# Seeds of a convolution kernel computed two eighths at a time, beside the attention projections

## The chip, the core and the metric

The kernel runs on one core of a Trainium2 chip. The time is device microseconds of one execution, from three runs. A profile comes from one further execution; its span is measured from the first to the last instruction, and its tables name the engines PE (matrix multiply), PEld (its weight loads), DVE (vector), ACT (scalar, activations), POOL (GpSimd) and SP, which here only issues transfers.

## The reference

The output is two results side by side. The first is an S4D convolution of `u` (2048 x 448) with a kernel made from 448 x 256 complex exponentials; the second is 16-head attention over 2048 positions with width 448.

```python
dt = exp(log_dt); A = -exp(log_A_real) + 1j * A_imag
C = (C_real + 1j * C_imag) * dt[:, None]
P = exp((A * dt[:, None])[:, :, None] * arange(L))
K = 2.0 * einsum("dn,dnl->dl", C, P).real
y = irfft(rfft(u.T, 2 * L) * rfft(K, 2 * L), 2 * L)[:, :, :L].T + u * D_skip
qkv = (x @ wqkv)...                          # H = 16 heads of 28
p = softmax(einsum("bhqd,bhkd->bhqk", q, k) * Dh ** -0.5)
b = einsum("bhqk,bhkd->bhqd", p, v) @ wo
out = concatenate([y, b], axis=-1)
```

## The kernel before

It has a first stage, in which a scheduler orders the instructions of each engine by priority and data, and a main stage, in which every engine keeps the order of the program. The main stage (scores, exponentials, products with `v`, and the convolution's matmuls and powers) is not touched by the change. In it `sdb` is the seeds of a block of 8 channels read back from memory, and each head group's first matmuls need the row maxima in `qhat`.

The first stage does two jobs side by side.

**The projections.** `work` is a list of 48 jobs: for each of four chunks `c` of 512 positions eight `qk_proj` (k and q of four head groups) and four `v_proj`, each 12 matmuls into one of three `pm` tiles. `transposes(c)` makes the four `xh` and `xl` of a chunk: PE transposes into `pt`, ACT copies `xh`, DVE subtracts for `xl`. `evac` empties a `pm` tile: ACT writes `hl`'s first half, DVE the second, and SP stores `hl` to `k` or `q` in memory; for k of the first two chunks `kb` and `dhl` follow on ACT, DVE and POOL, and for v ACT writes one of two `v` staging buffers. `project()` takes one job and first runs the evacuation of the job before, held in `pend`. The projection weights lie in the memory that later holds `khat`, so the `khat` loads follow the projections.

**The seeds.** `seeds(o)` makes the starting values of eighth `o` (of eight) of the exponentials `P`: it returns 13 lists of functions, one a slot. In order: `load` (four `nat` loads), `times_dt` on ACT, `exp_a`, `turn` (eight PE transposes into `pn`, ACT copies `tr`), `phases` (three small DVE operations on `pn`, one product over 128 x 1680 into `tri`, and one on POOL), `reduce` (two more such operations on DVE), `sines` (two sines, an absolute value and two cosines on ACT, into `sg` and `tri`), `sizes` (two exponentials on ACT), `factors` (three POOL operations on `sg`), `g_base` (two small POOL products on `tri`, then a negation on ACT), `e_all` (two POOL products from `tri` into a `qhat` buffer), `g_first` (nine DVE operations), `g_copies` (four small ACT copies), and the stores `put_e` (`sd<-qhat`) and `put_g` (`sd<-sg`). `tri` has two buffers, `sg` two and the `qhat` buffers three.

A loop over slots `t` interleaves both: eighth `o` begins at slot 4 `o` (`SP`), the projections are spread over 37 slots (`PW`), and `ahead` places the first `kdif`, `q` and `khat` loads. The 41 slots set the program order; the scheduler, whose priority follows it, sets the queues. After the loop come 16 steps that find the maxima of the first score tile (ACT `rl`, DVE, with `nq` from POOL), which need all `khat` and both parts of `qhat`; their PSUM tiles take the place of those of the first stage.

ACT needs a table load between a sine and an exponential. SP sends all transfers of this stage in one order; each of them takes one of eight semaphores in turn.

Of the kernel before, what the change touches and what calls it, by code (L numbers as in the profile page):

```python
# [8 lines left out]
F32 = mybir.dt.float32  # L9
F32R = mybir.dt.float32r  # L10
I32 = mybir.dt.int32
AF = mybir.ActivationFunctionType
ALU = mybir.AluOpType
# [25 lines left out]
S0, SP, SW, SD, PW, E3 = 0, 4, 0, 5, 37, 8  # L39
# [2 lines left out]
SGB, XB, XL = 2, 5, 4  # L42
K0, KP, KD, UP = 0, 3.5, 4, 3
A0, A1, KW = 26, 34, (33, 35, 36)

N1 = 32
N2 = 64
# [5 lines left out]
NO = 8  # L53
# [3 lines left out]
NF, NE = 6, 13  # L57
# [5 lines left out]
TWO_PI = 6.283185  # L63
# [28 lines left out]
def body(ctx, tc, a, out):  # L92
    nc = Engines(tc)
# [119 lines left out]
    with ExitStack() as st:  # L213
# [47 lines left out]
        t = a["A_log_dt"]  # L261
# [6 lines left out]
        half_pi = s_p.tile([128, 1], F32, name="half_pi")  # L268
# [42 lines left out]
        NH = BO * 16  # L311
        mul = lambda e, o_, x_, y_: e.tensor_tensor(o_, x_, y_, ALU.mult)

        def seeds(o):

            q = {}
            vec, pol, act = nc.vector, nc.gpsimd, nc.scalar
# [1 line left out]
            kb = lambda i: pw2[:, i, :, None].to_broadcast([128, LV, NH])  # L319

            def exp_a():
                act.activation(q["nat"][:, 0, :], q["nat"][:, 0, :], AF.Exp)

            def times_dt(i):
                n, d = q["nat"][:, i, :], dt_all[:, i or 4, o:o + 1]
                act.activation(n, n, AF.Copy, scale=d)
# [37 lines left out]
                q["g4"] = sg[:, :, :F_Z - F_G].rearrange("p b (c h e) -> p b c h e", c=2, e=4)  # L364
                q["f"] = sg[:, :, F_Z - F_G:].rearrange("p b (t k h) -> p t k b h", t=3, h=16)

            def both(t, i, *args, **kw):
                act.activation(q["f"][:, i], t[:, :NF].rearrange("p k (b h) -> p k b h", h=16), *args, **kw)
                act.activation(t[:, NF:], t[:, NF:], *args, **kw)

            def sines():
                f = q["f"][:, 2]
                act.activation(f, q["r"][:, :NF].rearrange("p k (b h) -> p k b h", h=16), AF.Sin, scale=TWO_PI)
                act.activation(q["sn"][:, NF:], q["r"][:, NF:], AF.Sin, scale=TWO_PI)
                act.activation(q["r"], q["r"], AF.Abs)
                both(q["r"], 0, AF.Sin, scale=-TWO_PI, bias=half_pi)

            def sizes():
                both(q["mg"], 1, AF.Exp)

            def factors():
                f = q["f"]
# [37 lines left out]
            put_e = lambda: nc.sync.dma_start(sd_d[o][:, :, :F_G].rearrange("b p f -> p b f"), q["se"])  # L420
            put_g = lambda: nc.sync.dma_start(sd_d[o][:, :, F_G:].rearrange("b p f -> p b f"), q["sg"])

            def load():
                if o not in nats:
                    load_nat(o)
                q["nat"] = nats.pop(o)
            dts = lambda *r: [lambda i=i: times_dt(i) for i in r]
            return [[load], dts(1, 2, 3), [], [exp_a] + dts(0), [turn, phases], [g_place, reduce], [sines], [sizes, places, g_base],
                    [e_all, g_first], [put_e, factors], [g_copies], [], [put_g]]

        xh, xl = {}, {}

        def transposes(c):
            for k in range(NCK):
                pt = ps_t.tile([128, CQ], F32, name="pt")[:CK]
                for t in range(4):
                    nc.tensor.transpose(pt[:, t * 128:(t + 1) * 128], xns[c, t // 2][:, t % 2, k * CK:(k + 1) * CK], ident)
                xh[k] = x_p.tile([CK, CQ], F32R, name="xh", bufs=XB)
                xl[k] = x_p.tile([CK, CQ], F32R, name="xl", bufs=XL)
                nc.scalar.activation(xh[k], pt, AF.Copy)  # L440
                nc.vector.tensor_tensor(xl[k], pt, xh[k].bitcast(F32), ALU.subtract)

        def qk_proj(c, s, g):
            pp = w_tile()
# [46 lines left out]
        for c in range(NQ):  # L491
            jobs = [lambda c=c, s=s, g=g: qk_proj(c, s, g) for g in range(G) for s in (1, 0)]
            v_jobs = [lambda c=c, t=t: v_proj(c, t) for t in range(4)]
            jobs = v_jobs + jobs if c == NQ - 1 else jobs + v_jobs
            jobs[0] = (lambda c, f: lambda: (transposes(c), f())[1])(c, jobs[0])
            if c + 1 < NQ:
                jobs[1] = (lambda c, f: lambda: (load_x(c + 1), f())[1])(c, jobs[1])
            work += jobs
        stages = [seeds(o) for o in range(NO)]
        n_stage = SP * (NO - 1) + len(stages[0])  # L500
        slots = [[] for _ in range(n_stage)]
        for o in range(NO):
            for i, st_ in enumerate(stages[o]):
                slots[max(SP * o + (i or -2), 0)] += st_
        slots[1].insert(0, turn_dt)
        pend, n_work = [], len(work)

# [9 lines left out]
        def project():  # L517

            e = work.pop(0)() if work else None
            while pend:  # L520
                pend.pop(0)()
            if e:
                pend.append(e)

        for t in range(n_stage):
            while work and n_work - len(work) < n_work * (t + 1) / PW:
                project()
            for f in slots[t] + ahead.get(t, []):
                f()
            if t + 1 == PW:  # L530
                project()
                wst.close()
                load_k(0, HG - 1, k0_p)
                load_q(1)
                for c in range(NQ):
                    load_v(0, c)
# [6 lines left out]
        for i in range(16):  # L543
            j, t = divmod(i, 4)
            ts = slice(t * 128, (t + 1) * 128)
            q, kt = q_u[0][:, j, ts], kt_g[0][j]
# [201 lines left out]
    def fin(u, s_):  # L748
# [15 lines left out]
        def scale():  # L764
            pw = w_tile()
            for t in range(4):
                nc.tensor.transpose(pw[:, t * 128:(t + 1) * 128], rb[:, t].rearrange("p h e -> p (h e)"), ident)
            nc.vector.tensor_tensor(on, o, pw, ALU.mult)
            if g < G - 1:
                nc.sync.dma_start(on_d[c][g], on)  # L770
            else:
                p_due.extend((s_ + PD + PS * t, lambda t=t: project(t)) for t in range(4))
# [385 lines left out]
```

## Time and profile before

| | us |
|---|---|
| three runs | 1304.3, 1303.38, 1303.45 (median 1303.45) |
| the profiled execution | 1307.74 |
| its span | 1305.7 |
| granted TensorE clock, mean | 0.976 |
| PE busy | 1228.7 (94%) |
| ACT busy | 980.3 (75%) |
| DVE busy | 907.0 (69%) |
| POOL busy | 865.9 (66%) |

Nearly all instructions are recorded at line 76, where a wrapper calls the engine, so groups are told apart by tile names: `pm` projection PSUM, `hl` and `kb` their evacuations, `tri`, `sg` and `pn` the seeds, `sd` the seeds in memory. A row of the timeline gives start, duration, engine, operation, output and inputs, and, where the engine had been idle, for how long and on whom it waited. A row of a group gives total busy time and the mean of one in ns, then the idle time before them. A row of the list of waits gives the total in us, the number of waits and the longest.

### The profile page before, as it was taken

Reading aid. Unit: us, or ns where it says so; the run is one execution under the profiler, and the core shown is the slowest. Engines: PE = TensorE matmul, PEld = TensorE weight load, DVE = VectorE, ACT = ScalarE, POOL = GpSimd, SP = SyncE. Lnnn points to the kernel's source line nnn. Section 1 sums busy time; section 2 is a strip of 40 time slices with the busy share of each in tenths; the row PEclk is TensorE's granted clock in tenths of the full one; section 3 lists DMA queues with packets and bytes.
Section 4 is the critical chain, followed back from the end, with each engine's and each line's share of the span. In section 5 each row is a group of like instructions: output and inputs, shape, how many; then the busy total and the mean of one; then the engine's idle time right before and its main releaser. Section 6 shows DMA issues by size and latency. Waiting matters only on the chain.

```text
span 1305.7 us, 32148 instructions
## 1 busy us (share of the span) xinstructions
PE 1228.7 (94%) x12193; PEld 695.7 (53%) x12193; DVE 907.0 (69%) x2001; ACT 980.3 (75%) x2046; POOL 865.9 (66%) x684
## 2 busy tenths in 40 slices
PE   6888877799999999999999999999997999999998
PEld 5766755355555555555555555555554555545333
DVE  5676656677777787777788888888986555636111
ACT  4877875588888888888788888888886666756463
POOL 2677654478888788888769999999995221424421
PEclk9989887799999999999999999999999999999999
DMA  6677679735866455468634232743324453647666
GB/s 202 207 273 257 218 259 271 212 66 136 185 147 142 109 149 157 142 169 231 162 104 105 56 83 62 157 111 78 82 59 139 146 158 136 203 142 238 202 161 175
DMA packets 200082, 205.28 MB, mean 157 GB/s; under 512 B 95992, under 2 KB 158520, under 8 KB 197880
## 3 DMA queue, kind: packets, MB, share of 16 engines
q1 hardware_dynamic: 199864, 203.22, 56.1%
q8 instruction: 96, 1.57, 0.5%
q14 instruction: 58, 0.48, 0.1%
q10 hardware_dynamic: 64, 0.02, 0.0%
HBM read 120.74 MB, written 82.18 MB: 155 GB/s over the span
## 4 chain that ended last, share of the span: by engine, by line
PE 72%; POOL 8%; ACT 7%; DVE 5%; DMA 4%; issue 4%; SPq 0%; ACTq 0%; POOLq 0%
PE pm L76 39%; PE pss L76 16%; PE po L76 16%; POOL sg L76 2%; POOL e L76 2%; DMA khat<-k 2%; POOL tri L76 2%; ACT tri L76 1%; ACT sg L76 1%; DVE mx L76 1%; POOL p L76 1%; ACT L76 1%; ACT p L76 1%; POOL eu L76 1%; DVE rl L76 1%
## 5 line engine op out<-in xcount | busy, mean ns | idle before, releaser
L76 ACT ACTIVATE p<-pss 128x512 f32<-128x512 f32 x1024 | 560.4, 609 | 109.9 <-PE pss L76 105.9
L76 PE MATMUL pss<-qhat,khat 128*128 128x512 f32 x1024 | 405.7, 402 | 4.0 <-DMA qhat<-mh 2.2
L76 DVE TENSOR_REDUCE mx<-pm 128x1 f32<-128x512 f32 x480 | 308.3, 683 | 121.2 <-PE pm L76 119.5
L76 PE MATMUL pm<-khat,qhat 128*128 128x512 f32 x720 | 314.4, 437 | 6.1 <-ACT rl L76 3.5
L76 POOL TENSOR_TENSOR e<-e,sdb 128x256 f32<-128x256 f32 x168 | 202.0, 1203 | 108.7 <-ACT e L76 67.2
L76 PE MATMUL po<-p,v 128*32 128x512 f32 x2048 | 271.0, 597 | 0.0
L76 POOL TENSOR_TENSOR e<-e,eu 128x256 f32<-128x256 f32 x168 | 248.3, 1478 | 13.2
L76 PEld LDWEIGHTS pm<-khat,qhat 128*128 128x128 f32 x720 | 135.4, 188 | 206.4 <-ACT p L76 47.0
L76 PEld LDWEIGHTS pss<-qhat,khat 128*128 128x128 f32 x1024 | 191.2, 189 | 52.5 <-ACT p L76 13.8
L76 DVE CUSTOM_DVE_ANT_0 rl<-pm,rl 128x512 f32<-128x512 f32 x240 | 165.3, 689 | 70.0 <-ACT rl L76 67.7
L76 POOL TENSOR_TENSOR eu<-e,sdb 128x256 f32<-128x256 f32 x168 | 202.3, 1204 | 0.0
L76 POOL TENSOR_TENSOR p<-pr,pr 64x448 f32<-64x448 f32 x64 | 73.2, 1144 | 155.6 <-PE pm L76 122.3
L76 DVE TENSOR_TENSOR g<-g,zg 128x128 f32<-128x128 f32 x392 | 162.0, 413 | 3.6
L76 ACT ACTIVATE rl<-pm 128x512 f32<-128x512 f32 x240 | 145.3, 605 | 7.7 <-issue 4.1
L76 PE MATMUL pm<-xh,khat 112*128 112x512 f32 x256 | 89.7, 431 | 19.6 <-DVE hl L76 10.6
L76 PE MATMUL pm<-kdif,qhat 128*128 128x512 f32 x240 | 97.0, 404 | 1.7 <-DVE pr L76 1.1
L76 DVE TENSOR_TENSOR zg<-g,zg 128x128 f32<-128x128 f32 x224 | 88.0, 393 | 5.3
L76 PEld LDWEIGHTS pm<-e,g 128*32 128x32 f32 x3584 | 56.9, 110 | 49.2 <-issue 15.7
L76 PE MATMUL pm<-e,g 128*32 128x64 f32 x3584 | 73.6, 223 | 8.7 <-POOL e L76 8.7
L76 ACT ACTIVATE y<-pm 128x448 f32<-128x448 f32 x48 | 26.5, 553 | 59.7 <-PE pm L76 39.1
L76 PEld LDWEIGHTS pm<-xh,khat 112*128 112x128 f32 x256 | 51.0, 205 | 35.9 <-DVE hl L76 12.6
L76 DVE TENSOR_TENSOR pr<-pm,ub 128x448 f32<-128x448 f32 x64 | 37.0, 619 | 46.9 <-PE pm L76 37.7
(133 smaller groups left out, 1491.6 us busy)
## 6 DMA issues: line engine op xcount, KB each, us to landing
sdb<-sd SPq DMA_DIRECT2D x56, 336.0 KB
khat<-k SPq DMA_DIRECT2D x64, 256.0 KB
qhat<-q SPq DMA_DIRECT2D x64, 256.0 KB
sd<-sg SPq DMA_DIRECT2D x8, 1456.0 KB
k<-hl SPq DMA_DIRECT2D x16, 512.0 KB
q<-hl SPq DMA_DIRECT2D x16, 512.0 KB
v<-v SPq DMA_DIRECT2D x32, 256.0 KB
mw<-in_mw SPq DMA_DIRECT2D x16, 512.0 KB
```

Source lines behind the costliest of these rows:

```text
L76: i = f(*args, **kw)
```

## The change

Four edits, all in the first stage.

Eighths now begin in pairs, at slots 0 and 1, 8 and 9, 16 and 17, 24 and 25; there are 38 slots in place of 41. Within an eighth the steps `g_place`, `places`, `sizes`, `g_first` and `put_g` change slots.

`in_group(g, i)` gives ACT's sines and exponentials numbers: `exp_a` of both eighths of pair p is group 3p, their sines and cosines 3p + 1, their `sizes` 3p + 2. Each instruction of a group gets an edge of order, without a semaphore, to every instruction of the group before it.

`transposes` issues `xh` and `xl` with a priority raised by 200, and so does `project()` with the pending evacuation. Nothing is computed otherwise than before.

```diff
+PRI = 200
...
+        groups = collections.defaultdict(list)
+        def in_group(g, i):
+            for b in groups[g - 1]:
+                tc.add_manual_dep(i.ins, b.ins.name, mybir.DependencyInfo(mybir.DependencyClass.NoSync, mybir.DependencyReason.DATA),
+                                  reason="one function table at a time")
+            groups[g].append(i)
...
-                act.activation(q["nat"][:, 0, :], q["nat"][:, 0, :], AF.Exp)
+                in_group(3 * (o // 2), act.activation(q["nat"][:, 0, :], q["nat"][:, 0, :], AF.Exp))
...
-            def both(t, i, *args, **kw):
-                act.activation(q["f"][:, i], t[:, :NF].rearrange("p k (b h) -> p k b h", h=16), *args, **kw)
-                act.activation(t[:, NF:], t[:, NF:], *args, **kw)
+            def both(n, t, i, *args, **kw):
+                g = 3 * (o // 2) + n
+                in_group(g, act.activation(q["f"][:, i], t[:, :NF].rearrange("p k (b h) -> p k b h", h=16), *args, **kw))
+                in_group(g, act.activation(t[:, NF:], t[:, NF:], *args, **kw))
...
-                act.activation(f, q["r"][:, :NF].rearrange("p k (b h) -> p k b h", h=16), AF.Sin, scale=TWO_PI)
-                act.activation(q["sn"][:, NF:], q["r"][:, NF:], AF.Sin, scale=TWO_PI)
+                in_group(g, act.activation(f, q["r"][:, :NF].rearrange("p k (b h) -> p k b h", h=16), AF.Sin, scale=TWO_PI))
+                in_group(g, act.activation(q["sn"][:, NF:], q["r"][:, NF:], AF.Sin, scale=TWO_PI))
                 act.activation(q["r"], q["r"], AF.Abs)
-                both(q["r"], 0, AF.Sin, scale=-TWO_PI, bias=half_pi)
+                both(1, q["r"], 0, AF.Sin, scale=-TWO_PI, bias=half_pi)
...
-                both(q["mg"], 1, AF.Exp)
+                both(2, q["mg"], 1, AF.Exp)
...
-            return [[load], dts(1, 2, 3), [], [exp_a] + dts(0), [turn, phases], [g_place, reduce], [sines], [sizes, places, g_base],
-                    [e_all, g_first], [put_e, factors], [g_copies], [], [put_g]]
+            return [[load], dts(1, 2, 3), [], [exp_a] + dts(0), [turn, phases], [reduce], [g_place, sines], [places], [sizes, g_base],
+                    [e_all], [put_e, factors, g_first], [g_copies], [put_g]]
...
-                nc.scalar.activation(xh[k], pt, AF.Copy)
-                nc.vector.tensor_tensor(xl[k], pt, xh[k].bitcast(F32), ALU.subtract)
+                with tc.high_priority(offset=PRI):
+                    nc.scalar.activation(xh[k], pt, AF.Copy)
+                    nc.vector.tensor_tensor(xl[k], pt, xh[k].bitcast(F32), ALU.subtract)
...
-        n_stage = SP * (NO - 1) + len(stages[0])
+        begin = [2 * SP * (o // 2) + o % 2 for o in range(NO)]
+        n_stage = begin[-1] + len(stages[0])
...
-                slots[max(SP * o + (i or -2), 0)] += st_
+                slots[max(begin[o] + (i or -2), 0)] += st_
...
-            while pend:
-                pend.pop(0)()
+            with tc.high_priority(offset=PRI):
+                while pend:
+                    pend.pop(0)()
```

More of the change, by code (lines that the diff above doesn't have):

```diff
@@ L365, in g_place @@
                 q["f"] = sg[:, :, F_Z - F_G:].rearrange("p b (t k h) -> p t k b h", t=3, h=16)
-            def both(t, i, *args, **kw):
-                act.activation(q["f"][:, i], t[:, :NF].rearrange("p k (b h) -> p k b h", h=16), *args, **kw)
-                act.activation(t[:, NF:], t[:, NF:], *args, **kw)
+            def both(n, t, i, *args, **kw):
+                g = 3 * (o // 2) + n
+                in_group(g, act.activation(q["f"][:, i], t[:, :NF].rearrange("p k (b h) -> p k b h", h=16), *args, **kw))
+                in_group(g, act.activation(t[:, NF:], t[:, NF:], *args, **kw))
             def sines():
-                f = q["f"][:, 2]
-                act.activation(f, q["r"][:, :NF].rearrange("p k (b h) -> p k b h", h=16), AF.Sin, scale=TWO_PI)
-                act.activation(q["sn"][:, NF:], q["r"][:, NF:], AF.Sin, scale=TWO_PI)
+                f, g = q["f"][:, 2], 3 * (o // 2) + 1
+                in_group(g, act.activation(f, q["r"][:, :NF].rearrange("p k (b h) -> p k b h", h=16), AF.Sin, scale=TWO_PI))
+                in_group(g, act.activation(q["sn"][:, NF:], q["r"][:, NF:], AF.Sin, scale=TWO_PI))
                 act.activation(q["r"], q["r"], AF.Abs)
-                both(q["r"], 0, AF.Sin, scale=-TWO_PI, bias=half_pi)
+                both(1, q["r"], 0, AF.Sin, scale=-TWO_PI, bias=half_pi)
             def sizes():
-                both(q["mg"], 1, AF.Exp)
+                both(2, q["mg"], 1, AF.Exp)
             def factors():
```

## The prediction

> **What bounds the kernel now.** I read the page's head first, then the windows of busy time, the chain of waits around 240 us, the list of who waited for whom up to there, and last the timelines of single queues.
>
> ```profile
> span 1305.7 us, 32148 instructions
> 0.00:208.00 208.00, 164.68 (x706) 128.74 (x707) 133.41 (x218) 146.46 (x254) 124.71 (x103) 0.92 0.73 237
> 208.00:242.00 34.00, 26.79 (x86) 17.31 (x84) 21.78 (x39) 16.91 (x17) 5.28 (x4) 0.80 1.00 286
> 245.00:1305.00 1060.00, 1035.16 (x11398) 548.18 (x11397) 751.81 (x1745) 816.91 (x1775) 735.90 (x578) 0.99 0.52 137
> ```
>
> A window row gives its length, the busy time of PE, weight loads, DVE, ACT and POOL, then the granted clock, the DMA share and GB/s. From 245 us on PE is busy 1035 of 1060 us. That part keeps its program order on every engine, so I carry it over unchanged: the change is worth what it does to the moment at which that part can start. In the first 208 us no engine is full (PE 79%, ACT 70%, DVE 64%, POOL 60%): something hands work round among them. Between 208 and 242 the DMA engines are: share 1.00 at 286 GB/s.
>
> ```profile
> 218.32 10.46 DMA khat<-k
> 236.38 5.56 DMA qhat<-mh
> 242.00 2.99 DMA sdb<-sd
> ...
> 232.66 0.37 SPq L76 DMA_DIRECT2D sd<-qhat  x1
> 233.82 0.37 SPq L76 DMA_DIRECT2D sd<-sg  x1
> ```
>
> The chain says the same: the main loop starts at 245 when the first `sdb` has landed. That load was issued at 242.00, once the last seed store (sent at 233.82, behind the `khat`, `qhat` and `v` loads in SP's queue) had landed. The score maxima reach their row of `qhat` at 241.9, so two paths end together. Both hang on a backlog of transfers that begins when the last seeds and projections are done.
>
> ```profile
> DVE hl L76 <- ACT hl L76: 27.5, 14, 5.3
> DVE sg L76 <- POOL tri L76: 23.2, 7, 5.5
> ACT tri L76 <- POOL tri L76: 21.4, 11, 3.7
> ...
> 33.55 1.91 DVE L76 TENSOR_TENSOR tri<-pn,pw 128x1680 f32<-128x1680 f32 x1
> ...
> 78.83 1.91 DVE L76 TENSOR_TENSOR tri<-pn,pw 128x1680 f32<-128x1680 f32 x1
> ...
> 121.69 1.91 DVE L76 TENSOR_TENSOR tri<-pn,pw 128x1680 f32<-128x1680 f32 x1
> ...
> 162.34 1.89 DVE L76 TENSOR_TENSOR tri<-pn,pw 128x1680 f32<-128x1680 f32 x1
> ```
>
> Two things wait in those 208 us. Projection evacuations wait for ScalarE (27.5 us), and the seeds' chain goes DVE, ACT, POOL, DVE. The four starts are eighths 0, 2, 4 and 6; the gaps are 45.3, 42.9 and 40.7 us for two eighths, which overlap because they are half a period apart.
>
> **The change part by part.** *Table loads.* ScalarE's queue has 17 now and 9 after.
>
> ```profile
> L76 ACT ACT_TABLE_LOAD x17 | 21.8, 1283 | 1.0 <-PEq L1148 0.7
> ...
> 170.82 0.77 ACT L76 ACTIVATE sg<-tri 128x672 f32<-128x672 f32 x1
> ...
> 175.73 1.12 ACT L76 ACTIVATE tri<-tri,half_pi 128x1008 f32<-128x1008 f32 x1
> ...
> 201.43 0.56 DVE L76 TENSOR_TENSOR sg<-pn,tri 128x224 f32<-128x224 f32 x1 [2.12 <-POOL tri L76]
> ...
> 205.06 0.55 DVE L76 TENSOR_TENSOR sg<-sg,px 128x224 f32<-128x224 f32 x1
> ```
>
> That frees 8 x 1.283 = 10.3 us of ScalarE. But ScalarE idles 21.4 us for POOL's `tri`, so this counts only where ScalarE's sequence sets the pace; one load remains in each pair's chain and is charged below. The Trainium skill, page "ScalarE: Activation LUTs", section "What ACT_TABLE_LOAD costs", puts a switch at 1283 ns plus a 1380 ns drain, 2.66 us. By that the eight would be 21.3 us. The trace agrees with the load alone.
>
> *Pairs.* The `tri` tile has two buffers. Now both hold eighths of the same pair, in the same stage, so the next pair's first product on DVE waits for the whole pair. The order edges add that no exponential of a pair runs before both its eighths' sines. In the changed program's queues a pair is one chain, whose terms are these rows:
>
> ```profile
> L76 POOL TENSOR_TENSOR qhat<-tri 128x784 f32<-128x784 f32 x16 | 29.8, 1869 | 0.0
> L76 POOL TENSOR_TENSOR sg<-sg 128x672 f32<-128x672 f32 x16 | 27.5, 1722 | 24.6 <-ACT sg L76 21.4 <-DVE pn L76 3.0
> ...
> L76 DVE TENSOR_TENSOR tri<-tri 128x1680 f32<-128x1680 f32 x8 | 21.1, 2640 | 0.1
> L76 POOL TENSOR_SCALAR sg<-sg 128x672 f32<-128x672 f32 x8 | 16.7, 2090 | 0.6
> ...
> L76 DVE TENSOR_TENSOR tri<-pn,pw 128x1680 f32<-128x1680 f32 x8 | 15.2, 1905 | 0.2
> L76 DVE SCALAR_TENSOR_TENSOR tri<-tri,pn 128x1680 f32<-128x1680 f32 x8 | 15.2, 1900 | 0.1
> ...
> L76 DVE SCALAR_TENSOR_TENSOR hl<-pm,kones,hl 128x512 fp32r<-128x512 f32 x16 | 11.9, 744 | 16.4 <-ACT hl L76 16.2
> L76 DVE TENSOR_TENSOR hl<-pm,hl 128x512 fp32r<-128x512 f32 x16 | 11.0, 687 | 11.4 <-ACT hl L76 11.2
> ...
> L76 DVE TENSOR_TENSOR xl<-pt,xh 112x512 fp32r<-112x512 f32 x16 | 10.8, 686 | 10.0 <-ACT xh L76 8.8 <-PE pm L76 1.2
> L76 POOL TENSOR_TENSOR tri<-tri 128x224 f32<-128x224 f32 x16 | 10.7, 670 | 17.0 <-ACT tri L76 16.9
> ...
> L76 POOL TENSOR_TENSOR dhl<-kb,dhl 128x256 fp32r<-128x256 f32 x8 | 8.2, 1020 | 6.7 <-ACT dhl L76 5.3 <-ACT tr L76 1.5
> ...
> L76 DVE TENSOR_TENSOR kb<-pm,kb 128x256 f32<-128x256 f32 x8 | 3.3, 414 | 0.5 <-ACT kb L76 0.5
> ...
> 58.52 4.21 DMA v<-v
> ```
>
> (1) DVE, first eighth: 1.905 + 1.900 + 2.640 = 6.45, and the evacuations queued between, 0.744 + 0.414 + 0.687: 8.3. (2) DVE, second eighth: three operations on half the columns of the 201.43 row, an estimate of 0.8; 6.45; three `xl` at 0.686: 9.3. (3) ScalarE, the second eighth's sines, two evacuations among them: 170.82 to the end of the 175.73 row, 6.0. (4) One load and the first exponential, which has the shape of the 170.82 row: 2.05. (5) POOL until the second eighth's `tri`: in pair 1, 2 x 1.722 + 2 x 0.670 + 2 x 1.869 + 2.090 + 1.722 + 2 x 0.670 = 13.7. (6) DVE's nine products, 201.43 to 205.61, 4.2; the next small ones 0.8; two `hl` 1.4: 6.4. Pair 1 also waits for its `xl` inputs, 3 x 8.8/16 = 1.7: 47.4 in all. The new waits have followers: behind each negation on ScalarE, which waits for POOL's `tri`, stand evacuations and the next pair's `nat` scalings; PE's transposes wait for those scalings, and the projections in PE's queue for the transposes. That is how a late POOL delays the next pair and the matmuls together.
>
> Pair 0 differs. POOL's queue has the first eighth's scaling ahead of its `tri`, both `sg` products of the second and two `dhl`: 17.4. ScalarE's sines stand behind four `v` evacuations with two staging buffers; a store took 4.21 us to land and I charge 3, between nothing and 4.2. DVE has 8.8 in (6), with four products of the first eighth and one evacuation round more. Sum: 8.3 + 9.3 + 9.0 + 2.05 + 17.4 + 8.8 = 54.8. Pair 2 has no `kb`, 12.0 in (5) and four `hl` in (6): 7.9 + 9.3 + 6.0 + 2.05 + 12.0 + 7.9 = 45.1. In pair 3 SP's queue needs `sd<-qhat` of eighth 7, so POOL counts through its `qhat`: 7.9 + 8.0 + 5.0 + 2.05 + 15.7 = 38.7. From 33.5: 33.5 + 54.8 + 47.4 + 45.1 + 38.7 = 219.5 us.
>
> *Priority.* It moves the evacuations ahead of seeds on ACT and DVE; those are the extras in (1) to (3) and (6). It removes waits of the 27.5 us row, so the projections end sooner. I cost that gain at nothing, because SP's queue covers it: after the last `q` store come eight small `kdif` loads and one `khat` block, then the two `sd<-qhat` of eighths 6 and 7, and only behind them three `khat` blocks, `sd<-sg`, the second `qhat`, `v` and the last `sd<-sg`. If that cover is gone, the projections' end decides and the gain is up to rival A's.
>
> *The backlog.* What stands in the queue from the last `sd<-qhat` on:
>
> ```profile
> khat<-k SPq DMA_DIRECT2D x64, 256.0 KB
> qhat<-q SPq DMA_DIRECT2D x64, 256.0 KB
> sd<-sg SPq DMA_DIRECT2D x8, 1456.0 KB
> ...
> v<-v SPq DMA_DIRECT2D x32, 256.0 KB
> ...
> sd<-qhat SPq DMA_DIRECT2D x8, 896.0 KB
> ```
>
> 896 + 2 x 256 + 12 x 256 + 2 x 1456 + 4 x 256 + 3 x 256 = 9184 KB, 9.40 MB. At the 286 GB/s of the full window that is 32.9 us: the last seed store lands at 219.5 + 32.9 = 252.4, against 242.0. POOL's `nq` and the maxima run beside it. So the main loop starts 10.4 us later: a span of 1316.1 against 1305.7. The profiled execution took 1307.74 us, 2.0 around its span, and the median of the runs is 1303.45; I add the same 10.4 to that: 1313.9.
>
> **The rivals.** *A, faster: the extras don't queue in the chain.* The evacuations fall into gaps where DVE and ACT wait anyway, and a pair takes what two eighths take now, 45.3, 42.9 and 40.7. Then the last `sd<-qhat` leaves at 33.5 + 128.9 + 38.7 = 201.1, the store lands at 234.0, and the time is 1303.45 - 8.0 = 1295.5. It decides from a mean interval of 45.6 us down: (242.0 - 32.9 - 38.7 - 33.5)/3. For it speak the idle times in the `hl` rows; against it, that sines, exponentials, POOL and products of a pair now follow one another. If instead the ten microseconds of table loads come out of today's path whole, 1303.45 - 10.3 = 1293.2, the same side. The same section of the Trainium skill asks to batch by set; its 21.3 us would make 1282.
>
> *B, worse: transfers hold the pairs back.* `sg` has two buffers, so a pair's sines wait until the last pair's stores have landed. One is 1.49 MB, 6.3 us at 237 GB/s, and SP sends it in order behind `hl`, `v` and `nat` transfers that themselves wait for engines. Three microseconds for each of three pairs make 1323. Also, DVE's longest step has no fixed length:
>
> ```profile
> 85.04 4.53 DVE L76 TENSOR_TENSOR tri<-tri 128x1680 f32<-128x1680 f32 x1
> ```
>
> It took 4.53 us there against the mean of 2.64, so it can stall, and both POOL products of a pair now run back to back beside it.
>
> *C, no change: later seeds and earlier projections cancel.* This needs the last `sd<-qhat` at 242.0 - 32.9 = 209.1 and gives 1303.
>
> **How the numbers follow.** My forecast has a chance of 0.55, B 0.20, A 0.19, C 0.06. A difference below 0.2%, 2.6 us, can't be told from none. Slower: the forecast and B, 0.75; within 0.2%: C, 0.06; faster: A, 0.19. The forecast alone spans 1306 to 1322, some 2 us on each of four stretches. The low end is A's 1295; the high end is B with the backlog at 237 GB/s, 39.7 us, so 6.8 more: 1330.
>
> **What would show it.** Nine table loads on ScalarE. The starts of DVE's `tri<-pn,pw` for eighths 0, 2, 4 and 6 near 33, 88, 136 and 181; starts 43 us apart would prove A. POOL's last `qhat<-tri` near 219, after the last `hl`, and SP's `sd<-qhat` right behind it. A window of full DMA of some 33 us after that, the first `sdb` load near 252, and an unchanged 1060 us from the start of the main loop. It is wrong if the `khat` loads go out before the seeds end, or if the main loop's length moves by more than 3 us.

## The result, and the profile after

| | before | after |
|---|---|---|
| median of four runs, us | 1303.41 (1302.62 to 1304.3) | 1325.74 (1323.04 to 1329.2) |
| the profiled execution, us | 1307.74 | 1327.18 |
| its span, us | 1305.7 | 1325.4 |
| granted TensorE clock, mean | 0.976 | 0.962 |
| first `e<-sdb` on ACT, us from the span's start | 245.15 | 266.00 |

The change makes the kernel slower, by a ratio of 1.0167 (95% interval 1.0152 to 1.0181), 22.3 us by the medians. The forecast was 1313.9.

The windows of busy time after, in the columns of the prediction's first fence:

```profile
0.00:208.00 208.00, 163.12 (x705) 129.68 (x705) 121.51 (x200) 127.75 (x228) 99.97 (x88) 0.88 0.67 224
208.00:242.00 34.00, 6.22 (x14) 4.47 (x15) 10.47 (x21) 12.16 (x21) 25.68 (x18) 0.50 0.77 198
245.00:1305.00 1060.00, 1036.07 (x11284) 553.32 (x11282) 766.36 (x1769) 827.02 (x1783) 733.23 (x577) 0.99 0.53 141
```

The third row is that of before within 1 us of PE. From the first `e<-sdb` to the end of the span it takes 1325.4 - 266.00 = 1059.4 us, against 1060.6 before. So the loss lies ahead of the main loop: its start moved by 20.9 us and its length by -1.2, 19.7 us of span between these two executions. The medians differ by 22.3, because the profiled execution of before lay 4.3 us above its median and that of after 1.4. In the first 208 us POOL is busy 99.97 us in place of 124.71 and VectorE 121.51 in place of 133.41: work was not added, it was reached later. Between 208 and 242, where before kept the DMA engines at a share of 1.00, POOL is the busy one (25.68 us) and the DMA share is 0.77.

The next fence holds rows of VectorE's timeline, the first products of eighths 0, 2, 4 and 6, so of the four pairs.

```profile
31.32 1.91 DVE L77 TENSOR_TENSOR tri<-pn,pw 128x1680 f32<-128x1680 f32 x1
...
84.73 1.89 DVE L77 TENSOR_TENSOR tri<-pn,pw 128x1680 f32<-128x1680 f32 x1
...
140.06 1.91 DVE L77 TENSOR_TENSOR tri<-pn,pw 128x1680 f32<-128x1680 f32 x1
...
188.76 1.90 DVE L77 TENSOR_TENSOR tri<-pn,pw 128x1680 f32<-128x1680 f32 x1
```

The pairs take 53.4, 55.3 and 48.7 us, where two eighths took 45.3, 42.9 and 40.7. What follows the last pair shows in SP's timeline:

```profile
210.53 1.80 SPq L77 DMA_DIRECT2D khat<-k  x4
220.77 0.39 SPq L77 DMA_DIRECT2D sd<-qhat  x1
227.49 0.38 SPq L77 DMA_DIRECT2D sd<-qhat  x1
229.74 2.28 SPq L77 DMA_DIRECT2D khat<-k  x4
232.12 0.38 SPq L77 DMA_DIRECT2D sd<-sg  x1
232.67 11.76 SPq L77 DMA_DIRECT2D khat<-k  x8
256.95 0.37 SPq L77 DMA_DIRECT2D sd<-sg  x1
259.98 7.38 SPq L77 DMA_DIRECT2D sdb<-sd  x3
```

After the first `khat` block SP stands for some 8 us in front of `sd<-qhat` of eighth 6, with twelve `khat` loads behind it. The last `sd<-qhat` leaves at 227.49 and the `sdb` loads 32.5 us later.

Last, the list of who waited for whom up to 260 us (total, times, longest) and POOL's timeline in pair 1:

```profile
POOL sg L77 <- ACT sg L77: 69.1, 4, 19.3
DVE sg L77 <- POOL tri L77: 50.0, 8, 13.4
```
```profile
95.83 3.00 POOL L77 TENSOR_TENSOR tri<-tr,pw 128x1680 f32<-128x1680 f32 x1 [1.40 <-ACT tr L77]
117.22 3.26 POOL L77 TENSOR_TENSOR sg<-sg 128x672 f32<-128x672 f32 x2 [18.39 <-ACT sg L77]
120.44 1.27 POOL L77 TENSOR_TENSOR tri<-tri 128x224 f32<-128x224 f32 x2
121.67 3.69 POOL L77 TENSOR_TENSOR qhat<-tri 128x784 f32<-128x784 f32 x2
```

Once a pair, four times in all, POOL has nothing to do for 14 to 19 us, because it waits for ScalarE's `sg`, the exponentials (18.39 in pair 1). Then it does both eighths' products in one piece, and VectorE waits for them: 50.0 us, where before the same row had 23.2.

### The profile page after: what moved, and what is told of

Read it like the earlier page. It is cut to its first block, busy times and chain, and to the rows that moved or that the text cites. A ratio compares the mean times of both kernels' runs of the same rounds, so it can differ in the third digit from the quotient of the medians.

```text
span 1325.4 us, 32153 instructions
## 1 busy us (share of the span) xinstructions
PE 1223.7 (92%) x12193; PEld 695.6 (52%) x12193; DVE 903.8 (68%) x2001; ACT 972.2 (73%) x2038; POOL 861.0 (65%) x684
## 4 chain that ended last, share of the span: by engine, by line
PE 73%; POOL 8%; issue 5%; DVE 5%; ACT 4%; DMA 3%; SPq 1%; ACTq 0%; POOLq 0%; DVEq 0%
PE pm L77 41%; PE pss L77 16%; PE po L77 15%; POOL sg L77 2%; POOL e L77 2%; DMA sd<-sg 1%; POOL qhat L77 1%; POOL tri L77 1%; DVE mx L77 1%; POOL p L77 1%; ACT tri L77 1%; DMA khat<-k 1%; ACT sg L77 1%; ACT p L77 1%; POOL eu L77 1%
## 5 line engine op out<-in xcount | busy, mean ns | idle before, releaser
L77 POOL TENSOR_TENSOR e<-e,eu 128x256 f32<-128x256 f32 x168 | 248.0, 1476 | 13.2
L77 PEld LDWEIGHTS pss<-qhat,khat 128*128 128x128 f32 x1024 | 191.1, 189 | 51.6 <-ACT p L77 13.6
L77 PEld LDWEIGHTS pm<-e,g 128*32 128x32 f32 x3584 | 56.8, 110 | 48.7 <-issue 16.1
L77 POOL TENSOR_TENSOR sg<-sg 128x672 f32<-128x672 f32 x16 | 26.1, 1645 | 69.1 <-ACT sg L77 69.1
```

The lines of the kernel that those rows point to most:

```text
L77: i = f(*args, **kw)
```

## The experiments

Four theories of the loss stood at the start. T1: two `tri` and two `sg` buffers held by one pair in one stage make the seeds' chain longer. T2: the fixed order of ScalarE's groups does it. T3: the priority does it. T4: the order of transfers in SP's queue does it. The twelve kernels ran in three sets, each beside the kernel before, whose median was 1304.14 in every set. For the later reading this table has three times from each trace: the last `hl` on VectorE, which ends the projections; the issue of the last `sd<-qhat`; and the first `e<-sdb`.

| kernel | time, us | ratio to before (95%) | table loads | last `hl` | last `sd<-qhat` | first `e<-sdb` |
|---|---|---|---|---|---|---|
| before (profiled run) | 1303.41 | | 17 | 207.4 | 232.7 | 245.2 |
| after | 1325.74 | 1.0167 (1.0152 to 1.0181) | 9 | 205.1 | 227.5 | 266.0 |
| priority alone | 1304.01 | 1.0003 (0.9990 to 1.0015) | 21 | 191.4 | 234.1 | 245.5 |
| after, no priority | 1325.59 | 1.0171 (1.0153 to 1.0189) | 9 | 225.0 | 221.8 | 264.4 |
| after, no edges | 1301.76 | 0.9982 (0.9972 to 0.9991) | 17 | 188.4 | 199.2 | 240.5 |
| pairs alone | 1319.64 | 1.0124 (1.0107 to 1.0140) | 15 | 220.9 | 214.7 | 258.7 |
| edges of `sizes` only | 1327.87 | 1.0179 (1.0158 to 1.0201) | 13 | 204.6 | 229.3 | 267.7 |
| the other edges only | 1301.95 | 0.9980 (0.9967 to 0.9993) | 17 | 190.6 | 201.3 | 242.7 |
| after, late stores | 1328.63 | 1.0179 (1.0156 to 1.0202) | 9 | 205.4 | 229.3 | 267.8 |
| no edges, late stores | 1305.39 | 1.0008 (0.9995 to 1.0020) | 17 | 190.3 | 213.3 | 245.6 |
| after, `g_base` on VectorE | 1311.67 | 1.0056 (1.0037 to 1.0076) | 9 | 189.1 | 213.9 | 252.3 |
| no edges, `g_base` on VectorE | 1298.05 | 0.9961 (0.9948 to 0.9974) | 17 | 184.4 | 194.1 | 236.6 |
| no edges, two slots apart | 1303.11 | 0.9993 (0.9983 to 1.0004) | 17 | 188.4 | 205.9 | 240.9 |
| no edges, half the priority | 1304.80 | 1.0006 (0.9994 to 1.0019) | 15 | 194.5 | 200.4 | 244.0 |

### First set: which of the three parts

**The priority alone**, on the kernel before:

```diff
-                nc.scalar.activation(xh[k], pt, AF.Copy)
-                nc.vector.tensor_tensor(xl[k], pt, xh[k].bitcast(F32), ALU.subtract)
+                with tc.high_priority(offset=PRI):
+                    nc.scalar.activation(xh[k], pt, AF.Copy)
+                    nc.vector.tensor_tensor(xl[k], pt, xh[k].bitcast(F32), ALU.subtract)
...
-            while pend:
-                pend.pop(0)()
+            with tc.high_priority(offset=PRI):
+                while pend:
+                    pend.pop(0)()
```

> The kernel before with only the raised priority of the evacuations (xh, xl and project's pending ones); eighths begin every four slots, no order edges. Theory T1 (the pairs make the seeds' chain longer, because both `tri` buffers and both `sg` buffers are held by one pair in one stage): about the time of before, 1296 to 1306, with starts of `tri<-pn,pw` for eighths 0, 2, 4 and 6 some 43 us apart. T2 (the fixed group order, exponentials only after both eighths' sines, makes it longer): the same 1296 to 1306. T3 (the priority pushes seed work back in ScalarE's and VectorE's queues): 1313 to 1326, with the four starts 47 us apart or more. T4 (the order of transfers in SP's queue costs it, seed stores ahead of the khat loads): here only the last eighth's stores stand behind all khat loads as in before, so about 1303.

1304.01, no difference, so T3 falls as the cause of the loss. Its mechanism is there all the same: the projections end 16 us sooner (191.4 against 207.4), and the last eighth's first `tri` product starts at 194.45 in place of 176.13. The last eighth's stores, which stand behind all `khat` loads here as before, leave at nearly the same time.

**After without the priority**, the same lines taken out of the changed kernel.

> The changed kernel without the raised priority: pairs and order edges stay. T1: 1318 to 1328, the four starts again some 50 us apart. T2: the same, 1318 to 1328. T3: 1300 to 1308. T4: seed stores of the last pair stand ahead of three khat blocks here too, so 1315 to 1326, and the projections should end later than 205 us.

1325.59, the time of after. With the edges in place the priority is worth nothing in either direction.

**After without the edges:**

```diff
-            for b in groups[g - 1]:
+            for b in ():
```

> The changed kernel without the order edges: pairs and priority stay, so ScalarE loads a table more often than 9 times. T1: 1318 to 1328 although up to 8 table loads (10 us of ScalarE) may come back. T2: 1300 to 1310, the four starts 43 us apart. T3: 1318 to 1328. T4: the order in SP's queue is that of the changed kernel, so 1315 to 1326 if the seeds end where they do now.

1301.76, not only 24 us less than after but 2.4 less than before, with eight more table loads than after. T2 is the only theory that had foreseen it; T1 and T3 had 1318 to 1328. T4 had 1315 to 1326 on the condition that the seeds end where they did in after, and they ended 28 us sooner, so this run does not test it. The same two rows of waits, and POOL in pair 1:

```profile
DVE sg L77 <- POOL tri L77: 17.3, 5, 4.9
...
POOL sg L77 <- ACT sg L77: 14.9, 5, 5.5
```
```profile
97.40 1.64 POOL L77 TENSOR_TENSOR sg<-sg 128x672 f32<-128x672 f32 x1 [0.24 <-ACT sg L77]
104.55 1.65 POOL L77 TENSOR_TENSOR sg<-sg 128x672 f32<-128x672 f32 x1 [5.51 <-ACT sg L77]
...
120.39 1.89 POOL L77 TENSOR_SCALAR sg<-sg 128x672 f32<-128x672 f32 x1
```

POOL starts the pair's `sg` products at 97.40 and has done all of the pair's work at 122.3. With the edges it could start only at 117.22.

**Pairs alone**, with neither edges nor priority.

> Only the pair starts and the moved steps: neither order edges nor priority. T1: 1315 to 1328, nearly the whole loss of 22. T2 and T3: each alone 1300 to 1308, since what each blames is gone. T4: 1315 to 1326, the last pair's stores again ahead of three khat blocks.

1319.64: T2 and T3 had 1300 to 1308 here, so the edges are not the only way to lose. The time lies in the ranges of T1 and T4, 1315 to 1328 and 1315 to 1326; T1 had missed the run before by 16 us. VectorE's timeline shows one thing that is late:

```profile
220.92 0.69 DVE L77 TENSOR_TENSOR hl<-pm,hl 128x512 fp32r<-128x512 f32 x1 [6.36 <-ACT hl L77]
```

The last evacuation is at 220.92 in place of 188.4: without the priority a pair's work pushes the projections back, and the `khat` loads need the projections' weight memory. The seeds are late too: the last `sd<-qhat` leaves at 214.7 in place of 199.2.

One path runs through all kernels of pairs with the stores in their place. Of the four loads of the first `qhat`, two stand in SP's queue behind the last `sd<-qhat` (with two slots apart, below, all stand ahead of it). The first product of the score maxima, `p` on PE, waits for these loads (at half the priority for a `khat` load). Sixteen steps on PE, ScalarE and VectorE follow, and the first `sdb` load leaves within 0.05 us of the end of VectorE's fifteenth maximum, `m`. In after, the last row being from SP's list of waits between 257.2 and 260.2 us:

```profile
235.41 0.77 PE L77 MATMUL p<-kdif,qhat 128*128 128x512 f32 x1 [38.02 <-DMA qhat<-q]
...
259.87 0.08 DVE L77 DVE_READ_ACCUMULATOR2_ANT m<- 128x1 f32 x1
...
SPq L77 <- DVE m L77: 1.7, 1, 1.7
```

From the last `sd<-qhat` it is 7.9 us to that product, 24.6 more to the `sdb` load and 6.0 more to the first `e<-sdb`; in the kernel without edges 10.8, 24.7 and 5.9. By the table the main loop starts 35 to 44 us behind the later of the projections' end and the last `sd<-qhat`.

Both parts move both ends. From the kernel without edges, the edges take the last `sd<-qhat` from 199.2 to 227.5 and the projections' end from 188.4 to 205.1; taking out the priority instead moves them to 214.7 and 220.9. With the edges in place the priority ends the projections 20 us sooner and lets the last `sd<-qhat` leave 6 us later, and the times are equal. This is as far as the runs explain why 18 us of the priority (1319.64 to 1301.76) show without the edges and none with them.

### Second set: which edges, and the order of transfers

T5 was formed here: the edges that hold the exponentials back starve POOL. T6: it is the edges between pairs. In **edges of `sizes` only** those of groups 3p + 2 stay; **the other edges only** is the counterpart.

```diff
-            for b in groups[g - 1]:
+            for b in groups[g - 1] if g % 3 == 2 else ():
```

> The changed kernel with only the edges of the groups 3p + 2 kept: a pair's exponentials of `sizes` after both eighths' sines; no order for the sines behind `exp_a` or for the next pair's `exp_a` behind the exponentials. T5 (these edges starve POOL: its first product of each pair waits for ScalarE's `sg`, 69.1 us of waits after against 14.9 without any edges, and both eighths' POOL work then runs in series behind them): 1319 to 1328, and the waits of POOL's `sg` for ScalarE's `sg` again 50 us or more. T6 (the other edges hold up the next pair's first ScalarE work): 1300 to 1306. Nine to eleven table loads under either.

> The counterpart: the edges of groups 3p and 3p + 1 kept (the next pair's `exp_a` after this pair's exponentials, sines after `exp_a`), those of 3p + 2 taken out, so that the first eighth's exponentials may come ahead of the second's sines. T5: 1299 to 1306, POOL's waits for ScalarE's `sg` below 25 us in all. T6: 1318 to 1328.

1327.87 and 1301.95: the whole loss against the kernel without edges is in the edges of `sizes`. The rows of waits, first with these edges, then with the others:

```profile
POOL sg L77 <- ACT sg L77: 63.8, 4, 21.4
DVE sg L77 <- POOL tri L77: 49.0, 8, 14.5
```
```profile
DVE sg L77 <- POOL tri L77: 17.6, 5, 5.0
...
POOL sg L77 <- ACT sg L77: 14.9, 5, 5.5
```

The number of table loads, 13 there and 17 here, was expected at nine to eleven and came out higher; it does not go with the time.

**Late stores**, on the changed kernel and on the one without edges:

```diff
+        held = []
...
-                    [e_all], [put_e, factors, g_first], [g_copies], [put_g]]
+                    [e_all], [put_e] * (o < NO - 2) + [factors, g_first], [g_copies], [put_g] * (o < NO - 2)]
...
                 load_k(0, HG - 1, k0_p)
+                for f, _ in held:
+                    f()
                 load_q(1)
...
+        for _, f in held:
+            f()
         xst.close()
```

`held` has `put_e` and `put_g` of eighths 6 and 7.

> The changed kernel with all edges, but the seed stores of eighths 6 and 7 issued behind the khat blocks (both `sd<-qhat` before the second `qhat`, both `sd<-sg` at the end). T4 (part of the loss is that SP's queue stood idle for the last seeds with three khat blocks behind them): behind the last `sd<-qhat` there remain 0.9 + 1.0 + 0.8 + 3.0 MB, about 5.7 MB or 20 us at 286 GB/s in place of 32.5 us, so about 12 us come back: 1310 to 1316. T5 in its plain form (the end of the seeds alone counts): 1322 to 1328.

> The kernel without edges (pairs and priority) with the same late seed stores. There the last `sd<-qhat` left at 199.2, only 6 us after the first khat block, so SP's queue hardly stood idle. T4 and T5 alike: 1296 to 1302, a gain of 0 to 5 over the 1301.8 without edges, because the projections end at 188 and khat could go out some microseconds earlier; more than 5 would say that transfers, not the seeds, are its bound.

Both missed. For the first T4 had 1310 to 1316 and T5 in its plain form 1322 to 1328, and 1328.63 came out; for the second both had 1296 to 1302, and it took 1305.39. All `khat` loads did go out from 210.8 to 228.3, yet the `sdb` loads left at 261.23, later than the 259.98 of after. Windows of the kernel with late stores, then one of after:

```profile
229.00:261.00 32.00, 23.23 (x83) 15.89 (x83) 20.31 (x36) 17.59 (x19) 9.61 (x7) 0.82 0.77 209
210.00:229.00 19.00, 1.19 (x2) 0.52 (x2) 8.18 (x18) 7.86 (x15) 16.02 (x12) 0.50 0.98 212
```
```profile
227.00:260.00 33.00, 23.39 (x80) 15.78 (x80) 20.03 (x34) 17.17 (x20) 11.38 (x8) 0.77 1.00 243
```

With the `khat` loads nearly by themselves the DMA share is 0.98 at only 212 GB/s; mixed, they move 243 GB/s. My 20 us for 5.7 MB had taken the 286 GB/s of another mixture. Why the rate differs with the mixture stays open. But behind the `khat` loads the share is 0.77, so from there on the DMA engines were not full. Two other rows of the kernel with late stores, one of PE's timeline and one of SP's list of waits, show what held it up:

```profile
234.40 0.80 PE L77 MATMUL p<-khat,nq 128*128 128x512 f32 x1 [10.30 <-POOL nq L77]
...
SPq L77 <- DMA qhat<-mh: 15.5, 1, 15.5
```

PE had its first `p` product at 222.90, 12.5 us sooner than in after, and then waited 10.30 us for `nq`, which POOL reaches only behind the last seeds. And SP, with the `sdb` loads behind the last `sd<-sg`, waited 15.5 us ahead of that store for the maxima's transfer `qhat<-mh`, because each transfer takes one of eight semaphores in turn and the store's was still held by that one. The kernel without edges and with late stores has the same wait with 8.1 us. So the edit gained on one wait and met two others. It shows that this order of transfers is no cure; what the order of after costs by itself, T4, these runs leave open.

### Third set: POOL in the pair's chain, and the pair's distance

T5 says that a pair's chain goes exponentials, POOL, VectorE. **`g_base` on VectorE** takes POOL out of one link:

```diff
-                mul(pol, q["r"][:, NE:], q["mg"][:, NE:], q["r"][:, NE:])
-                mul(pol, q["sn"][:, NE:], q["mg"][:, NE:], q["sn"][:, NE:])
+                mul(vec, q["r"][:, NE:], q["mg"][:, NE:], q["r"][:, NE:])
+                mul(vec, q["sn"][:, NE:], q["mg"][:, NE:], q["sn"][:, NE:])
```

> The changed kernel with all its edges, but the two small products of `g_base` (tri<-tri, 128x224) on VectorE in place of POOL. T5 says that a pair's chain runs exponentials, POOL, then VectorE's nine products; with this edit VectorE's products no longer wait for POOL (50.0 us of waits in 8 after), and what is left of POOL in the chain is that its `qhat` products free `tri` for the next pair. Expected: 5 to 15 us back, 1311 to 1321, with the waits of VectorE's `sg` for POOL's `tri` gone, and POOL's first product of a pair still 14 to 19 us late. If POOL's late work is off the chain (rival T7: the pair is held by ScalarE's and VectorE's own queues, or by PE's transposes), the time stays at 1323 to 1329.

> The same edit on the kernel without edges, where VectorE's `sg` waits only 17.3 us for POOL's `tri`. T5: at most a small gain, 1298 to 1302; T7: unchanged, 1301 to 1303. If VectorE is the tighter engine there, 1303 to 1306.

1311.67 and 1298.05, both as T5 had it; T7, under which the time would have stayed, falls. In the first, POOL still waits for the exponentials, but VectorE no longer waits for POOL:

```profile
POOL sg L77 <- ACT sg L77: 59.3, 4, 19.0
```

Its pairs take 49.9, 51.0 and 47.4 us and its tail 34.7 (starts of `tri<-pn,pw` at 31.00, 80.86, 131.85 and 179.27, last `sd<-qhat` at 213.93): 3.5, 4.3, 1.3 and 4.1 less than after, together 13.2 of the 14.1 us between the two times. The second is the fastest kernel of the study: 0.9961 of before (0.9948 to 0.9974), 6 us. Between the two the edges still cost 13.6 us. So POOL's link is a part of the loss and not all of it: with `g_base` on VectorE, VectorE itself waits 20.1 us for the exponentials (the row is in the last section).

**Two slots apart** is the kernel without edges with `begin = 2 * SP * (o // 2) + 2 * (o % 2)`; **half the priority** is the same kernel with `PRI = 100`.

> The kernel without edges, with the second eighth of a pair two slots behind the first in place of one. Between one slot (1301.8) and the four of the kernel with the priority alone (1304.0, which also has the older step lists) a theory that the two `tri` buffers in one stage cost time (T1, left over) expects less than 1301; the other theories expect 1300 to 1304, no difference that can be told.

> The kernel without edges with half the priority offset, 100. Pairs without edges took 1319.6 with no offset and 1301.8 with 200. If the offset works as a switch that lets evacuations past the seed steps of the same slots, 100 lies at either end: 1300 to 1304 or 1315 to 1320; a gradual effect would give about 1306 to 1313.

1303.11 and 1304.80. Neither helps. What was left of T1 is not seen: a pair one slot apart (1301.76) is no slower than two slots apart. Two slots apart the last `sd<-qhat` leaves 6.7 us later, but the first `qhat` loads stand ahead of it, and the main loop starts only 0.4 us later. At 100 the time lies between the range of a switch (to 1304) and that of a gradual effect (from 1306), and the projections end 6 us later than at 200 (194.5); this run does not decide between the two.

A third buffer for `tri` or `sg`, which would have tested T1 directly, was not tried; one more `tri` is 3 x 15 x 112 floats, 19.7 kB of each partition.

## Why the prediction was right in sign and half the size

Two steps failed. The sum of the pairs came out 8.0 us too small, mostly because what follows a late POOL was named and not priced. And the path from the last `sd<-qhat` to the main loop was not the one described; there one size agreed by luck and another was 2.9 us too small. Together they are the 10.5 us between the predicted start of the main loop, 245.15 + 10.4, and 266.00. The time lies above the 1306 to 1322 of the forecast alone, near rival B's 1323, but B's own mechanism, below, shows with only 1.9 us in pair 1.

**What bounds the kernel, and what the change can reach: right.** The main loop's length moved by 1.2 us, and nine table loads remain on ScalarE:

```profile
L77 ACT ACT_TABLE_LOAD x9 | 11.5, 1283 | 0.9 <-PEq L1162 0.7
```

**The backlog: the size agrees, the path was wrong.** From the last `sd<-qhat` to the `sdb` load it took 32.5 us, predicted 32.9. That is luck. The prediction had the load wait until the last seed store, `sd<-sg`, has landed, and read this out of before. SP's list of waits there, from 233.9 to 242.1 us, names the maxima's transfer:

```profile
SPq L76 <- DMA qhat<-mh: 7.7, 1, 7.7
```

In after the load waited for the fifteenth maximum, as shown above, and left 3.0 us after `sd<-sg` was sent, at 256.95. The window in between:

```profile
256.95:259.98 3.03, 2.49 (x10) 1.36 (x8) 3.01 (x6) 2.45 (x3) 0.00 (x0) 1.00 1.05 287
```

At 287 GB/s that is 0.87 MB in all, and the store has 1.49 MB: it can't have landed. So the 32.5 us are not 9.40 MB at 286 GB/s. They are 7.9 us until the first `qhat` is there and 24.6 us of maxima, which the prediction let run beside the transfers at no price. The `sdb` load then took 266.00 - 259.98 = 6.0 us until ScalarE could use it, 2.9 more than before; I had carried over the 3.1 of before. That the unfinished store ahead of it is the reason fits, but no run tests it. SP's three issues of `sdb` took 7.38 us in place of the 1.28 of before; 5.9 of these are the third load's wait for `qhat<-mh`.

**The pairs' sum: the terms that were mis-sized.** The last `sd<-qhat` was due at 219.5 and left at 227.49. Start and pair 0 came 2.2 and 1.4 us sooner than predicted, the tail came out at the predicted 38.7, and the excess is in pair 1 (55.3 against 47.4) and pair 2 (48.7 against 45.1). Pair 1 by its own steps, from four queues:

```profile
102.85 0.76 ACT L77 ACTIVATE sg<-tri 128x672 f32<-128x672 f32 x1 [2.71 <-DMA sd<-sg]
...
108.90 1.04 ACT L77 ACTIVATE tri<-tri 128x1008 f32<-128x1008 f32 x1
...
113.45 1.12 ACT L77 ACTIVATE tri<-tri,half_pi 128x1008 f32<-128x1008 f32 x1
...
115.08 1.28 ACT L77 ACT_TABLE_LOAD   x1
116.37 0.77 ACT L77 ACTIVATE sg<-tri 128x672 f32<-128x672 f32 x1
...
130.41 1.69 ACT L77 ACTIVATE nat<-nat,dt_all 56x256 f32<-56x256 f32 x4
...
138.31 0.26 ACT L77 ACTIVATE tr<-pn 128x112 f32<-128x112 f32 x1 [1.79 <-PE pn L77]
```
```profile
104.74 1.90 DVE L77 TENSOR_TENSOR tri<-tri 128x1680 f32<-128x1680 f32 x1
```
```profile
128.80 1.28 POOL L77 TENSOR_TENSOR tri<-tri 128x224 f32<-128x224 f32 x2
```
```profile
133.51 0.74 PE L77 MATMUL pm<-vh,xh 112*128 112x448 f32 x1 [4.04 <-DVE hl L77]
...
137.18 1.10 PE L77 MATMUL pn<-ident,nat 56*128 56x56 f32 x8
```

| step of pair 1 | predicted | measured | from, to |
|---|---|---|---|
| (1), (2) both eighths on VectorE, with the waits for `xl` | 8.3 + 9.3 + 1.7 | 21.9 | 84.73 to 106.64 |
| (3) the second eighth's sines | 6.0 | 7.9 | to 114.57 |
| (4) load and first exponential | 2.05 | 2.6 | to 117.14 |
| (5) POOL until the second `tri` | 13.7 | 12.9 | to 130.08 |
| (6) until the next pair's first product | 6.4 | 10.0 | to 140.06 |

Steps (4) and (5), the series that the order of exponentials makes, were sized rightly. The largest miss is step (6); in pair 2 it is 11.2 against 7.9 (177.60 to 188.76), nearly the whole of that pair's 3.6. I had counted only VectorE's own operations there. The prediction names, in the same paragraph, what else lies on the way, "behind each negation on ScalarE ... stand evacuations and the next pair's `nat` scalings; PE's transposes wait for those scalings", and gives it no price. The rows show it: ScalarE waits for POOL and then its scalings run from 130.41, PE's eight transposes come at 137.18, behind `v` matmuls that had themselves waited 4.04 us for VectorE's late `hl`, and `tr` at 138.31 ends the wait. The next miss, 2.6 us, is in steps (1) and (2): VectorE's waits there were 1.43 us for `hl`, 2.46 for PE ahead of the first `xl` and 1.31 for `xh`, where 1.7 in all was charged, while its two last steps took 1.91 and 1.90 us in place of the mean of 2.64. The miss of 1.9 us in step (3) is rival B's mechanism: the first eighth's sine waited 2.71 us for `sd<-sg` to leave its buffer, which pushed the second eighth's sines to 108.90, though VectorE was done at 106.64.

**The priority costed at nothing: right for this kernel**, 1325.59 without it against 1325.74. The text's proviso, that the projections' end decides if the cover is gone, fits the 18 us between the pairs alone and the kernel without edges, though there the seeds' stores moved by 15.5 us as well.

**Rival A** had 0.19 and its mechanism was spoken against by one argument only, that sines, exponentials, POOL and products of a pair follow one another. That is the edges' doing. Without them the last `sd<-qhat` left at 199.2 and the `sdb` loads at 234.6; A had worked out 201.1 and 234.0. Its time came out 1301.8, not 1295.5: the `sdb` load took 5.9 us there, 2.8 more than A had carried over. Most of the rest lies in the profiled execution of before, from which A counted: it was 3.6 us above the median of its set, that of the kernel without edges 0.8.

**Table loads as a gain.** The prediction let a load count only where ScalarE sets the pace. The runs agree: after with 9 loads is 24 us slower than its twin with 17. The Trainium skill, page "ScalarE: Activation LUTs", section "Table sets: the hidden batching unit", advises to do all calls of one set together; this is the section that has the advice, and not the one on what a load costs, to which the prediction pointed. In this kernel following it cost 24 us, because another engine waited for the exponentials; the freed 8 x 1.283 us lay beside that wait.

## What to carry to other kernels

Before grouping one engine's work by kind, ask who waits for its last group: an order that saves 10 us on ScalarE may let POOL run dry for 14 to 19 us each round, and POOL's work then stands in series with everything behind it. When a follower queued behind a wait is named, price it too: here the unpriced followers (scalings, transposes, a queue of matmuls) were the largest part of the error. Where a stage is said to wait for a transfer, look up in the list of waits which one, and whether the bytes could have moved by then; here a right number hid a wrong path. And test the parts of a change in combinations: the priority was worth 0, 0 or 18 us, depending on the other parts.

## What the runs showed of the hardware

VectorE's operations with both inputs in SBUF have no fixed length. The last product of `reduce` took 4.53 us beside a POOL product in the prediction's row. By groups, in the kernel before and in the one with `g_base` on VectorE and edges:

```profile
L76 DVE TENSOR_TENSOR tri<-tri 128x1680 f32<-128x1680 f32 x8 | 21.1, 2640 | 0.1
L76 DVE SCALAR_TENSOR_TENSOR tri<-tri,pn 128x1680 f32<-128x1680 f32 x8 | 15.2, 1900 | 0.1
```
```profile
L77 DVE TENSOR_TENSOR tri<-tri 128x224 f32<-128x224 f32 x16 | 21.5, 1375 | 20.1 <-ACT tri L77 20.1
L77 DVE TENSOR_TENSOR tri<-tri 128x1680 f32<-128x1680 f32 x8 | 15.2, 1902 | 0.1
```

The large step takes 1.90 us in the second kernel, where POOL mostly waits meanwhile, as long as the one with an input in PSUM took in both; in before it averaged 2.64. In two rows it went by which of the two began first. The 4.53 us began at 85.04, behind a POOL product of 3.00 us that had begun at 84.80. In after the large step began at 91.92, just ahead of POOL's `dhl` product, and took 1.91 us; the `dhl` product took 2.48 us, where another like it (83.04) took 0.73. The small `g_base` products, which run beside POOL's products into `sg` and `qhat`, took 1.375 us on VectorE on average, though operations on the same 128x224 with an input in PSUM took 0.37 to 0.59; on POOL, in after, they had taken 0.664. So part of what the move saves is paid in this way. The Trainium skill, page "GPSIMD Engine Reference", section "1. Specifications", says that GpSimd shares its SBUF interfaces with VectorE and contends with instructions that have two SBUF inputs; these rows agree.
